# A new written order of all steps for a fused gated-attention and spatial-gating kernel on one core

## The chip, the core and the metric

The kernel runs on one core of a Trainium2 chip. The metric is the device time of one execution in microseconds (us); several runs are made and their median is compared. The core has a matrix engine (TensorE, PE in the profile; its weight loads are the separate row PEld), a vector engine (VectorE, DVE), an activation engine (ScalarE, ACT), a general one (GpSimd, POOL) and a queue engine (SyncE, SP) that issues all transfers here.

## What is computed

The first half is a gated linear attention over 4 batches, 8 heads, 768 tokens and 48 columns a head. The second half works on its output x, 768 tokens by 384 columns for each batch:

```python
f = 1 / (1 + exp(-f_logit))
for t in range(S):
    state = f[t][:, None] * state + outer(k[t], v[t])
    y[t] = q[t] @ state
h = relu(x @ w_in); u, v = h[..., :512], h[..., 512:]
v_n = (v - mean(v)) / sqrt(var(v) + 1e-6)
v_s = w_spatial @ v_n + b_spatial
out = (u * v_s) @ w_out
```

## The kernel before

The attention is cut into 24 units, numbered n = 0 to 23, of 128 tokens for all 8 heads: six units to a batch. The second half is cut by batch b, by half th of the tokens (384 each), by unit u inside the batch, and by column block c of 128. Every product in the second half is made as three products of a high and a low part (hi by hi and the two mixed ones).

The program is fully unrolled. Its order is a written list, PLAN, of 1176 steps; each step is a small function that issues one or a few instructions on one engine or one transfer on SP. Every engine works through its own instructions strictly in the order of the list, and waits by semaphores for what it needs from the others. So the list sets, for each engine, what stands behind what. A second list, BESIDES, names steps that take the other of two variants: c, r2 go to GpSimd instead of VectorE; sm goes to VectorE instead of GpSimd; ys goes to VectorE instead of ScalarE; for V, U, S and P it only swaps the second and third of the three products.

The steps that the texts below name, with their lines:

- Transfers on SP: LF:n gate logits of unit n (192 KB for the first eight units, L353, all of f, k and q, 768 KB, later), LK:n keys and queries (512 KB, L359), LQ:n values (192 KB, L363), LV and LU halves of w_in (768 KB, L294).
- Unit n: c (clamp, L367), e (exp and log, ACT L371 and L372), z (running sums: 16 matmuls for n under 8, L382, a DVE scan from n = 8), h and g (exponentials, ACT L388 and L393), k and q (scaled keys and queries, DVE L399 and L403), X (32 matmuls, scores and state update weights, L427), w (ACT copy, L433), m (DVE mask, L437), YS and kv (32 matmuls each, L479 and L451), r0, r1, r2 (state, L459, L465, L470), Yq (16 or 32 matmuls, L491), ys (output copy, L495), xt (3 transposes, L504), xh and xl (high and low part of x, ACT L515 and DVE L520).
- Weights: ca (ACT L303), ct (three DVE instructions, L308 to L310), ch and cl (high and low part, ACT L314 and DVE L320) turn words of a weight into two parts.
- Second half: V and U (9 matmuls each, L542 and L644), vr, bs, na, nb, nc, vn, vh, vl (normalisation; vl is the low part of v_n, L634), wh and wl (parts of w_spatial), S (18 matmuls, L658), P (the same product by sums of blocks for batches 2 and 3, 9 matmuls, L733), sm, sh, sl (gating and its parts), O (12 matmuls, L797), oc and od (copy out and store).

The tiles that bind the early transfers are few: three buffers `ins` for f, k, q of a unit, two `vals`, two `words`. LF:3 waits until k:0 and g:0 have read the f of buffer 0; LF:4 likewise for k:1; LK:3 waits for X:0; LQ:2 for kv:0. SP issues in list order, so one that waits holds all behind it.

Two lines of the loop that runs a step and of the variant test:

```python
def beside(name, *at):
    return name + ":" + ",".join(str(x) for x in at) in BESIDES
...
for what in PLAN[:stop]:
    ...
    run(what)
```

Of the kernel before, what the change touches and what calls it, by code (L numbers as in the profile page):

```python
# [29 lines left out]
P = 128  # L30
# [30 lines left out]
    xl:8 ch:O,1 r1:9 z:10 cl:O,1 bs:1,1 e:11 h:10 g:10 LW:2,1 sg:0,0,1 wh:2,1 wl:2,1 z:11 sm:0,0,1 sh:0,0,1 S:0,0,0  # L61
    k:10 sg:0,0,0 fm:9 r2:9 h:11 g:11 LF:12 q:10 k:11 S:0,0,2 sg:0,0,2 LW:1,1 wh:1,1 wl:1,1 bs:1,0 V:1,2 vr:1,2
    bs:1,2 na:1,0 X:10 w:10 LF:13 Yq:9 U:0,1,0 LQ:10 sl:0,0,1 m:10 q:11 sm:0,0,3 S:0,1,0 sg:0,1,0 ys:9 c:12 ur:0,1,0
    fm:11 sh:0,0,3 YS:10 sl:0,0,3 X:11 m:11 e:12 LF:14 nb:1,0 w:11 kv:10 LQ:12 xt:9 nc:1,0 r0:10 ur:0,0,2 xh:9 r1:10
    z:12 LO:0 r2:10 sm:0,0,0 S:0,1,3 sm:0,0,2 sg:0,1,3 vn:1,0 sh:0,0,0 sl:0,0,0 S:0,1,1 sg:0,1,1 sh:0,0,2 fm:10 h:12
    g:12 U:0,1,1 ur:0,1,1 sl:0,0,2 k:12 Yq:10 ys:10 c:13 e:13 YS:11 kv:11 r1:11 fm:12 q:12 X:12 LF:15 w:12 xl:9
    r0:11 c:15 z:13 m:12 h:13 Yq:11 ca:O,0 fm:13 xt:10 vn:1,2 ys:11 g:13 q:13 sm:0,1,0 S:0,1,2 YS:12 kv:12 c:14 e:14
    k:13 X:13 e:15 r0:12 Yq:12 xh:10 xt:11 xh:11 sg:0,1,2 ct:O,0 ch:O,0 xl:10 LQ:14 U:0,1,2 xl:11 cl:O,0 ur:0,1,2
    sm:0,1,2 sh:0,1,0 V:1,4 w:13 vh:1,2 r1:12 r2:12 z:14 h:14 fm:14 mr1 LQ:13 m:13 sm:0,1,1 O:0,0,0 oc:0,0,0
    od:0,0,0 vh:1,0 O:0,0,2 oc:0,0,2 g:14 k:14 O:0,0,1 YS:13 ys:12 od:0,0,2 sm:0,1,3 q:14 X:14 vl:1,2 vn:1,1 vh:1,1  # L70
    vl:1,1 m:14 sh:0,1,2 sl:0,1,2 sl:0,1,0 kv:13 V:1,5 vr:1,5 V:1,3 oc:0,0,1 vl:1,0 z:15 xt:12 sh:0,1,3 sl:0,1,3
    U:1,0,2 vr:1,4 r0:13 sh:0,1,1 bs:1,5 sl:0,1,1 O:0,1,2 bs:1,4 r1:13 r2:13 vr:1,3 xh:12 xl:12 O:0,1,0 w:14
    ur:1,0,2 LQ:15 O:0,1,1 bs:1,3 na:1,1 nb:1,1 nc:1,1 vn:1,3 vn:1,4 LF:16 c:16 h:15 g:15 k:15 vh:1,4 vh:1,3 Yq:13
    q:15 YS:14 ys:13 kv:14 r0:14 vn:1,5 vh:1,5 X:15 LF:18 vl:1,5 Yq:14 ys:14 oc:0,1,2 vl:1,3 vl:1,4 S:1,0,3 sg:1,0,3
    w:15 e:16 r1:14 r2:14 z:16 h:16 g:16 fm:16 S:1,0,2 LF:17 c:17 e:17 LQ:16 S:1,1,3 k:16 oc:0,1,0 sg:1,0,2 q:16
    U:1,0,3 ur:1,0,3 m:15 X:16 sg:1,1,3 m:16 fm:15 YS:15 kv:15 r0:15 r1:15 r2:15 U:1,0,0 ur:1,0,0 Yq:15 od:0,0,1
    z:17 S:1,1,2 S:1,0,1 U:1,0,1 w:16 h:17 g:17 sm:1,0,2 ys:15 k:17 oc:0,1,1 c:18 e:18 q:17 LF:19 sm:1,0,3 c:19 e:19
    z:19 sg:1,1,2 mr0 fm:17 h:19 X:17 w:17 ur:1,0,1 z:18 sh:1,0,2 sg:1,0,1 sm:1,0,1 sh:1,0,1 YS:16 kv:16 xt:13 xh:13
    r0:16 r1:16 r2:16 h:18 xl:13 g:18 LQ:17 xt:14 m:17 xt:15 S:1,0,0 k:18 Yq:16 q:18 YS:17 g:19 xh:14 ys:16 kv:17
    xl:14 X:18 r0:17 m:18 r1:17 Yq:17 sl:1,0,1 q:19 ys:17 U:1,1,2 xh:15 xl:15 k:19 ur:1,1,2 sm:1,1,2 w:18 S:1,1,0  # L80
    sg:1,1,0 LF:21 fm:18 c:21 sg:1,0,0 sm:1,0,0 sh:1,0,0 X:19 w:19 LQ:18 YS:18 kv:18 r0:18 r1:18 fm:19 xt:16 xt:17
    sh:1,1,2 xh:17 r2:18 sl:1,0,0 od:0,1,2 xl:17 od:0,1,0 sh:1,0,3 sl:1,0,3 S:1,1,1 sg:1,1,1 LF:20 e:21 xh:16 c:20
    LQ:20 m:19 e:20 z:20 V:2,0 h:20 fm:20 g:20 vr:2,0 sl:1,0,2 O:1,0,0 oc:1,0,0 k:20 LQ:19 xl:16 O:1,0,1 od:0,1,1
    LF:22 c:22 Yq:18 ys:18 sl:1,1,2 YS:19 kv:19 q:20 X:20 r0:19 Yq:19 r1:19 e:22 r2:19 LF:23 z:21 w:20 O:1,0,2 h:21
    g:21 U:1,1,1 ur:1,1,1 k:21 U:1,1,3 ur:1,1,3 U:1,1,0 fm:21 sm:1,1,3 z:22 sh:1,1,3 q:21 ys:19 ur:1,1,0 m:20 X:21
    c:23 e:23 oc:1,0,2 sm:1,1,0 m:21 z:23 sh:1,1,0 oc:1,0,1 YS:20 kv:20 LQ:21 V:2,1 vr:2,1 r0:20 r1:20 sl:1,1,3
    r2:20 w:21 bs:2,1 bs:2,0 V:2,2 h:22 fm:22 vr:2,2 g:22 k:22 U:2,0,1 ur:2,0,1 Yq:20 sm:1,1,1 YS:21 kv:21 LQ:23
    ys:20 q:22 X:22 r0:21 Yq:21 bs:2,2 na:2,0 sh:1,1,1 xt:19 xh:19 xl:19 xt:20 sl:1,1,1 xh:20 nb:2,0 nc:2,0 vn:2,2
    vh:2,2 vl:2,2 od:1,0,0 V:2,5 vr:2,5 r1:21 r2:21 V:2,3 vr:2,3 LQ:22 sl:1,1,0 h:23 O:1,1,0 xl:20 w:22 fm:23 bs:2,5
# [921 lines left out]
```

## Time and profile before

| quantity | value |
| --- | --- |
| median of three runs (lowest, highest) | 344.14 us (343.51, 344.34) |
| time of the profiled execution | 343.65 us |
| span of the profiled execution, first to last instruction | 341.9 us |
| PE busy | 327.2 us (96%) |
| DVE, ACT, POOL busy | 251.3, 181.9, 48.2 us |
| granted PE clock over the span | 0.997 |

The chain of waits gives start, length and what ran, as it ended last. A timeline row gives start, length, engine, line and the operation, with its output and input; x is how many instructions were merged, and brackets hold the idle time before and what ended it. A stretch row gives its bounds and length, then for each engine the busy time and in brackets the number of instructions, then the granted clock, the share of time that the DMA engines moved data, and GB/s. "issue" is time in which the engine waited for nothing that the profile shows. Queue q1 carries the transfers that SP issues; queue q8 carries packets of instructions.

### The profile page before, as it was taken

To read this page: it belongs to the slowest core of one execution; us is meant where nothing else is said; L and a number is where in the kernel's file an instruction comes from. 1 tells how busy PE (TensorE), PEld (TensorE's weight loads), DVE (VectorE), ACT (ScalarE), POOL (GpSimd) and SP (SyncE) were. 2 spreads that over 40 slices of the span, in tenths; PEclk is the share of its full clock that TensorE was granted. 3 is DMA by queue.
4 is the path that set the end of the run, shared out by engine and by line. 5 is a ranking of instruction groups with operands and counts; after the bars stand their busy time and mean duration, and the time that the engine had idled before them with its cause. 6 is when DMAs were issued, how large, how long until landed. Compare 5 with 4: busy or idle time off the path is not lost.

```text
span 341.9 us, 10491 instructions
## 1 busy us (share of the span) xinstructions
PE 327.2 (96%) x4554; PEld 304.7 (89%) x4554; DVE 251.3 (74%) x491; ACT 181.9 (53%) x369; POOL 48.2 (14%) x70
## 2 busy tenths in 40 slices
...
GB/s 253 353 97 269 182 271 304 252 30 138 143 157 134 83 54 110 77 157 117 2 143 265 46 85 50 46 200 104 71 1 0 2 0 0 2 46 49 23 74 98
DMA packets 16582, 38.38 MB, mean 112 GB/s; under 512 B 1552, under 2 KB 11792, under 8 KB 16528
## 3 DMA queue, kind: packets, MB, share of 16 engines
...
q14 instruction: 16, 0.13, 0.1%
HBM read 32.90 MB, written 4.72 MB: 110 GB/s over the span
## 4 chain that ended last, share of the span: by engine, by line
PE 93%; DMA 2%; issue 1%; DVE 1%; ACT 1%; SPq 0%; DVEq 0%
PE mm L658 15%; PE mm L644 12%; PE mm L542 12%; PE mm L797 10%; PE mm L733 7%; PE mn L733 6%; PE bp L427 6%; PE mn L797 5%; PE bp L479 4%; PE bp L491 4%; PE mn L542 3%; PE mn L644 3%; PE mm L504 3%; PE bp L451 3%; DMA words<-w_cv 2%; PE mm L382 2%
## 5 line engine op out<-in xcount | busy, mean ns | idle before, releaser
L399 DVE SCALAR_TENSOR_TENSOR fkq<-fkq 112x512 f32<-112x512 f32 x24 | 17.2, 718 | 11.4 <-ACT fkq L393 6.9
L649 ACT ACTIVATE uT<-mm 128x384 f32<-128x384 f32 x26 | 12.8, 491 | 22.8 <-PE mm L644 19.9
L779 ACT CAST gh<-uT 128x384 fp32r<-128x384 f32 x29 | 14.8, 514 | 18.3 <-DVE uT L775 13.6
L427 PE MATMUL bp<-q,fkq 48*64 48x112 f32 x768 | 23.7, 261 | 0.8 <-DVE q L403 0.6
L775 POOL TENSOR_TENSOR uT<-gt,uT 128x384 f32<-128x384 f32 x12 | 12.9, 1077 | 81.1 <-ACT uT L649 38.6
L470 POOL TENSOR_TENSOR sA<-sA,F 112x192 f32<-112x192 f32 x13 | 11.9, 916 | 85.4 <-DVE sA L465 81.2
L427 PEld LDWEIGHTS bp<-q,fkq 48*64 48x64 f32 x768 | 19.0, 133 | 4.7 <-DVE q L403 1.9
L377 DVE TENSOR_TENSOR_SCAN fkq<-runs,fkq 112x512 f32<-112x512 f32 x16 | 20.4, 1274 | 2.8 <-ACT fkq L372 2.8
L479 PEld LDWEIGHTS bp<-val,sc 64*64 64x64 f32 x768 | 14.2, 134 | 7.4 <-issue 3.5
L479 PE MATMUL bp<-val,sc 64*64 64x48 f32 x768 | 16.6, 220 | 4.1 <-DVE sc L437 2.1
L403 DVE TENSOR_TENSOR q<-fkq,F 112x512 f32<-112x512 f32 x24 | 16.5, 686 | 5.4 <-PE bp L491 4.0
L658 PE MATMUL mm<-w_sph,vnh 128*128 128x384 f32 x96 | 20.2, 345 | 0.0
L658 PE MATMUL mm<-w_sph,vnl 128*128 128x384 f32 x96 | 19.5, 338 | 0.0
L658 PE MATMUL mm<-w_spl,vnh 128*128 128x384 f32 x96 | 19.5, 338 | 0.0
L437 DVE TENSOR_TENSOR sc<-bp,mask 128x512 f32<-128x512 f32 x24 | 16.4, 683 | 3.8 <-PE bp L427 3.7
L644 PE MATMUL mm<-xTh,w_inh 128*128 128x384 f32 x78 | 18.9, 350 | 0.0
L367 POOL TENSOR_SCALAR fkq<-fkq 112x512 f32<-112x512 f32 (+1 forms) x8 | 12.4, 1550 | 40.7 <-DMA fkq<-fkq 20.6
L644 PE MATMUL mm<-xTl,w_inh 128*128 128x384 f32 x78 | 17.9, 338 | 0.0
L644 PE MATMUL mm<-xTh,w_inl 128*128 128x384 f32 x78 | 17.9, 338 | 0.0
L542 PE MATMUL mm<-w_inh,xTh 128*128 128x512 f32 x57 | 17.3, 411 | 0.0
L658 PEld LDWEIGHTS mm<-w_spl,vnh 128*128 128x128 f32 x96 | 17.1, 188 | 0.0
L658 PEld LDWEIGHTS mm<-w_sph,vnl 128*128 128x128 f32 x96 | 17.1, 188 | 0.0
(215 smaller groups left out, 900.3 us busy)
## 6 DMA issues: line engine op xcount, KB each, us to landing
...
val<-vv SPq DMA_DIRECT2D x24, 192.0 KB, 4.0
out<-osb SPq DMA_DIRECT2D x24, 192.0 KB, 2.1
fkq<-fkq SPq DMA_DIRECT2D x8, 512.0 KB, 5.7
...
fkq<-fn SPq DMA_DIRECT2D x8, 192.0 KB, 3.4
...
```

The costliest lines, as they stand in the source:

```text
L377: return nc.vector.tensor_tensor_scan(f[0:DP], runs, f[0:DP], 0.0, op0=ALU.mult, op1=ALU.add)
L399: nc.vector.scalar_tensor_tensor(k, f, 1.0 / F_LEAST, k, op0=ALU.min, op1=ALU.mult)
L403: nc.vector.tensor_tensor(qs[n % 2][:, :, :, 0:C], *(x.rearrange("p (j c t) -> p j c t", c=T // C, t=C) for x in (parts(n)[2], Fs[n % 2])) ...
L427: nc.tensor.matmul(sc[to, e, cs], k[dr, at:at + C], qs[n % 2][dr, j, chunk], start=True, stop=True)
L437: nc.vector.tensor_tensor(Ss[n % 2].rearrange("p (e j t) -> p e j t", e=2, t=C), scores(n)[:, :, :, 0:C], mask.unsqueeze(1).unsqueeze(1).b ...
L479: nc.tensor.matmul(y[to, e, cs], s[rows, keys[e]], v[rows, hd], start=j == 0, stop=False, skip_group_check=True)
L542: nc.tensor.matmul(acc, xs[:, c, ut * P:(ut + 1) * P], ws[:, c, G:FF], start=i == 0, stop=i == 3 * KX - 1)
L644: nc.tensor.matmul(acc[:, 0:TH], ws[:, kx, cs], xs[:, kx, :], start=i == 0, stop=i == 3 * KX - 1)
L658: nc.tensor.matmul(acc[:, 0:TH], vns.of((b, ks))[va][:, cs], w_sp_s[wb][:, ks, th * TH:(th + 1) * TH], start=i == 0, stop=i == 3 * KS - 1,)
L733: nc.tensor.matmul(mm.of(user)[:, 0:TH], x, y, start=n == ks == 0 and i not in (3, 6, 7), stop=n == ks == 2, skip_group_check=True,)
L779: nc.scalar.copy(gs.take((b, th, c), HU)[0], uTs.of((b, th, c)))
L797: nc.tensor.matmul(acc[:, ms], gs.of((b, th, c))[ga][:, ts], w_out_s[wb][:, c, ms], start=c == cs[0] == 0 and ga == wb == 0, stop=c == cs[ ...
```

## The change

Only the two lists change. The steps are the same 1176; their order is new from the beginning to the end, and 75 names in BESIDES differ (42 only before, 33 only after). In the first microseconds: LV:1, the first half of w_in for v, is issued as the fourth transfer instead of the fifth, ahead of LF:2; LQ:1 goes ahead of LQ:0, LK:2 ahead of LV:0, LK:3 behind LF:4; Yq:0 goes ahead of X:1 on PE; c:2 goes from POOL to DVE, ahead of ct:V,1; ys:0 from ACT to DVE. Up to V:0,2 the order on PE is otherwise unchanged.

```diff
 PLAN = """
-    LF:0 constants kz LF:1 kq:1 c:0 e:0 LF:2 kq:0 c:1 LK:0 e:1 z:0 g:0 k:0 h:0 q:0 c:2 kj e:2 LV:1 z:1 LQ:0 ca:V,1
-    ct:V,1 X:0 w:0 h:1 g:1 LK:1 z:2 ch:V,1 m:0 k:1 YS:0 kv:0 q:1 LF:3 c:3 e:3 LV:0 r0:0 r1:0 X:1 w:1 cl:V,1 g:2 r2:0
-    Yq:0 z:3 fm:0 h:2 LQ:1 m:1 YS:1 kv:1 LK:3 LK:2 ys:0 k:2 q:2 ca:V,0 xt:0 X:2 LF:4 c:4 r0:1 LQ:2 r1:1 xh:0 xl:0
-    e:4 z:4 m:2 g:3 LF:5 w:2 LK:4 r2:1 c:5 e:5 YS:2 kv:2 LQ:4 Yq:1 fm:1 h:3 ct:V,0 ys:1 ch:V,0 r0:2 q:3 z:5 g:5 g:4
-    k:3 xt:1 LQ:3 LU:0 r1:2 cl:V,0 r2:2 xh:1 xl:1 X:3 w:3 Yq:2 ys:2 V:0,1 k:4 fm:2 h:4 LF:7 LF:6 q:4 X:4 m:3 YS:3
-    c:6 kv:3 V:0,0 LK:5 ca:U,0 LU:1 ct:U,0 r0:3 w:4 ch:U,0 vr:0,1 xt:2 xh:2 m:4 YS:4 fm:3 r1:3 e:6 r2:3 vr:0,0 kv:4
-    h:5 Yq:3 LQ:6 xl:2 V:0,2 fm:5 ys:3 xt:3 z:6 c:7 cl:U,0 e:7 r0:4 k:5 ca:U,1 vr:0,2 q:5 X:5 LQ:5 r1:4 w:5 LK:6
...
+    LF:0 constants c:0 kz kq:1 e:0 kq:0 LF:1 z:0 c:1 e:1 h:0 fm:0 z:1 LK:0 q:0 g:0 k:0 X:0 LV:1 ca:V,1 LF:2 c:2 e:2
+    ct:V,1 h:1 fm:1 LK:1 w:0 LQ:1 m:0 z:2 LQ:0 YS:0 kv:0 q:1 g:1 k:1 LF:3 c:3 LK:2 g:2 r0:0 Yq:0 ch:V,1 X:1 e:3 z:3
+    cl:V,1 r1:0 LV:0 r2:0 LF:4 ca:V,0 c:4 h:2 fm:2 ys:0 m:1 YS:1 k:2 LK:3 LQ:2 LF:5 w:1 q:2 kv:1 r0:1 r1:1 r2:1 xt:0
+    xh:0 xl:0 X:2 e:4 m:2 LK:4 w:2 c:5 z:4 YS:2 kv:2 LQ:4 h:3 fm:3 LU:0 ct:V,0 Yq:1 e:5 z:5 g:3 k:3 ys:1 q:3 xt:1
+    r0:2 r1:2 ch:V,0 X:3 LQ:3 xh:1 Yq:2 cl:V,0 xl:1 g:4 k:4 r2:2 LF:7 V:0,1 w:3 ys:2 h:4 LK:5 ca:U,0 q:4 LF:6 X:4
+    m:3 YS:3 ct:U,0 w:4 kv:3 r0:3 g:5 r1:3 LU:1 V:0,0 xt:2 m:4 YS:4 kv:4 fm:4 LQ:6 ch:U,0 vr:0,1 cl:U,0 vr:0,0 xh:2
+    Yq:3 LQ:5 r2:3 h:5 c:6 fm:5 c:7 r0:4 e:6 r1:4 xl:2 e:7 V:0,2 ys:3 ca:U,1 vr:0,2 z:6 r2:4 h:6 q:5 z:7 LK:6 h:7
+    fm:6 fm:7 k:5 ct:U,1 X:5 Yq:4 w:5 m:5 LF:8 g:6 xt:3 k:6 ys:4 g:7 U:0,0,0 c:8 nm:0,0 YS:5 q:6 kv:5 X:6 r0:5 Yq:5
...
-    bs:0,5 na:0,1 k:9 fm:8 V:1,0 xt:7 xh:7 xl:7 wh:2,0 nb:0,1 LO:1 ca:O,1 U:0,1,3 nc:0,1 vn:0,4 X:9 vh:0,4 w:9
-    vn:0,3 YS:8 kv:8 r0:8 vl:0,4 V:1,1 m:9 vh:0,3 vl:0,3 LW:1,0 wh:1,0 vr:1,0 c:11 vn:0,5 vh:0,5 YS:9 kv:9 LQ:11
-    wl:1,0 Yq:8 ys:8 wl:2,0 r1:8 moe vr:1,1 vl:0,5 ur:0,1,3 S:0,0,3 r2:8 xt:8 r0:9 sg:0,0,3 e:10 ct:O,1 S:0,0,1 xh:8
...
+    U:0,0,2 k:9 wl:0,1 q:9 X:9 nb:0,1 xh:7 LW:1,0 nc:0,1 w:8 xl:7 vn:0,3 vh:0,3 m:9 LQ:9 vn:0,5 LB V:1,1 LF:11
+    wh:1,0 fm:9 w:9 vn:0,4 YS:8 wl:2,0 vh:0,4 kv:8 wl:1,0 moe YS:9 kv:9 r0:8 vh:0,5 Yq:8 vl:0,5 vl:0,4 vl:0,3
+    S:0,0,0 vr:1,0 LO:1 ca:O,1 e:10 c:11 ct:O,1 vr:1,1 z:10 r1:8 ch:O,1 cl:O,1 fm:8 sg:0,0,0 ys:8 sm:0,0,0 S:0,0,3
...
 BESIDES = """
-    c:2 r2:0 r2:1 r2:2 c:6 V:0,0 ys:5 U:0,0,1 U:0,0,3 V:0,4 c:10 V:0,5 U:0,0,2 r2:7 V:1,1 r2:8 S:0,0,1 sm:0,0,1
-    S:0,0,0 r2:9 U:0,1,0 sm:0,0,3 S:0,1,0 c:15 sm:0,1,0 U:0,1,2 r2:12 sm:0,1,1 r2:13 ys:14 r2:14 S:1,1,3 S:1,1,2
...
+    r2:0 c:4 ys:0 r2:1 r2:2 ys:4 c:8 V:0,3 r2:6 U:0,0,1 V:0,4 V:0,5 U:0,0,3 c:9 r2:7 V:1,1 S:0,0,0 sm:0,0,0 S:0,0,3
+    r2:8 sm:0,0,3 r2:9 S:0,0,1 S:0,1,1 S:0,1,0 sm:0,0,1 c:13 U:0,1,1 r2:10 sm:0,1,1 S:0,1,3 ys:11 U:0,1,2 sm:0,1,3
...
```

## Rows read from the trace of the kernel before

**Rows 1.** The page's busy time, share of the span and instructions by engine.
```profile
PE 327.2 (96%) x4554; PEld 304.7 (89%) x4554; DVE 251.3 (74%) x491; ACT 181.9 (53%) x369; POOL 48.2 (14%) x70
```

**Rows 2.** The chain of waits, first 80 us: start, length, what ran.
```profile
2.65 7.09 DMA words<-w_cv
...
17.55 1.64 issue
...
23.69 0.39 issue
...
26.74 0.99 PE bp L427 x32
...
32.55 0.47 issue
...
37.37 2.29 PE mm L542 x9
...
74.19 3.37 PE mm L658 x18
```

**Rows 3.** Stretches: PE, PEld, DVE, ACT, POOL busy and count, clock, DMA, GB/s.
```profile
10.00:20.00 10.00, 6.12 (x220) 5.08 (x212) 8.16 (x14) 6.58 (x12) 1.22 (x2) 1.00 0.79 286
20.00:30.00 10.00, 8.94 (x240) 7.37 (x238) 8.77 (x16) 7.65 (x16) 1.84 (x4) 1.00 0.47 150
...
0.00:17.50 17.50, 9.88 (x221) 8.16 (x221) 9.84 (x19) 13.02 (x24) 4.56 (x15) 1.00 0.84 299
...
19.10:24.00 4.90, 3.90 (x126) 3.20 (x127) 3.92 (x8) 3.33 (x8) 0.65 (x2) 1.00 0.50 152
```

**Rows 4.** The timeline of PE around its first pauses.
```profile
13.37 0.68 PE L479 MATMUL bp<-val,sc 64*64 64x48 f32 x32 [2.08 <-DVE sc L437]
...
17.11 0.43 PE L479 MATMUL bp<-val,sc 64*64 64x48 f32 x13
19.18 0.49 PE L479 MATMUL bp<-val,sc 64*64 64x48 f32 x18 [1.64 <-issue]
```

**Rows 5.** DMA queues in 13:16.9, 16.92:17.93, 20:21.7, 21.7:22.65 us: packets, MB, share.
```profile
q1 hardware_dynamic: 604, 1.50, 99.3%
...
q8 instruction: 1, 0.02, 6.2%
...
q1 hardware_dynamic: 156, 0.53, 98.4%
...
q8 instruction: 1, 0.02, 6.1%
```

**Rows 6.** DMA share, 24 to 27 us in 40 slices; the lone 9 is q8.
```profile
DMA  0000000000000000900000004488967674630010
```

**Rows 7.** The timeline of SP: the transfers issued around two pauses.
```profile
10.33 0.80 SPq L359 DMA_DIRECT2D fkq<-fkq  x2
...
18.27 0.33 SPq L353 DMA_DIRECT2D fkq<-fn  x1
18.70 0.38 SPq L359 DMA_DIRECT2D fkq<-fkq  x1
```

**Rows 8.** DMA issues at 1.72 and 2.18 us: count, KB, us to landing.
```profile
fkq<-fn SPq DMA_DIRECT2D x1, 192.0 KB, 3.4
...
fkq<-fkq SPq DMA_DIRECT2D x1, 512.0 KB, 5.6
```

**Rows 9.** The timeline of DVE from the first conversion of w_in.
```profile
9.77 0.56 DVE L308 TENSOR_SCALAR words<-words 128x768 int32<-128x768 int32 x1 [0.28 <-DMA words<-w_cv]
10.74 0.98 DVE L309 SCALAR_TENSOR_TENSOR words<-words 128x768 int32<-128x768 int32 x1 [0.41 <-ACT words L303]
...
12.63 0.68 DVE L437 TENSOR_TENSOR sc<-bp,mask 128x512 f32<-128x512 f32 x1
...
14.43 0.35 DVE L367 TENSOR_SCALAR fkq<-fkq 128x384 f32<-128x384 f32 x1
```

**Rows 10.** DVE alone, 9.77 to 76.20 us: length, busy time, count.
```profile
9.77:76.20 66.43, 58.45 (x112) 1.00 0.65 220
```

More of the change, by code (lines that the diff above doesn't have):

```diff
@@ L60 @@
-    wl:1,0 Yq:8 ys:8 wl:2,0 r1:8 moe vr:1,1 vl:0,5 ur:0,1,3 S:0,0,3 r2:8 xt:8 r0:9 sg:0,0,3 e:10 ct:O,1 S:0,0,1 xh:8
[L61 to L89, printed above, removed]
```

99 lines of the change are left out of this document (63 added, 36 removed).

## The prediction

> **What bounds the kernel now.** Begin with the busy times: PE works 327.2 us [rows 1] of a span of 341.9, so 14.7 us are all that an order can win as long as the matmuls stay the same. The stretches say where these lie: from 10 to 20 us PE idles 3.9 us, from 20 to 30 us 1.1 us [rows 3]; the first 4.9 us wait for the first input and some 3.8 us at the end for the last stores, and both lists keep these. After 33 us PE is busy without a break, so what is won before then is won at the end, if nothing new waits later. The chain of waits then shows what PE's early idle time is. Three pieces of it are "issue": 1.64 us at 17.55, 0.39 at 23.69, 0.47 at 32.55 [rows 2]. In the timeline of PE the first lies in the middle of YS:1, after 13 of its matmuls [rows 4]: no data can be missing there, since the same step went on before and after it.
>
> The instruction queue explains it. From the start to that pause PE runs 221 matmuls and as many weight loads, and from there to the next pause some 126 of each [rows 3], so pauses come at every 128 or so. A packet of q8 lies ahead of each: 16.92 to 17.93 us, and 21.7 to 22.65 [rows 5]; PE goes on 1.25 us after the first has ended and 1.4 after the second (at 19.18 and 24.08). So PE's instructions come in blocks, and PE stops where the next is not there yet.
>
> When is a block asked for? If two blocks lie ready, then when PE steps from one into the next: for the first at 221 - 128 = 93 matmuls, the first ones of YS:0, about 13.6 us; for the second at 19.18; for the third at 24.08. The packets start 3.3, 2.5 and 1.1 us later. The third met an empty queue [rows 6]; ahead of the first two the transfers keep the DMA engines at 99% and 98% [rows 5]. I read this as a wait behind what SP had issued before: LK:3 and LK:2, 512 KB each, issued from 10.33 us, for the first; LF:5 and LK:4, issued at 18.27 and 18.70, for the second [rows 7].
>
> The Trainium skill, page "Runtime: NRT & Kernel Launch", section "Instruction fetch mechanics", describes blocks of 16 KiB, but calls the crossing of a boundary mostly hidden and gives PE room for 2,048 instructions. The trace disagrees here: 1.64 us stand open after 442. By the page nothing would be won there, and the sum below would be 0.35 us in place of 1.9.
>
> Behind PE stands DVE: from 9.77 to 76.20 us, where the sixth vl of batch 0 is done, it works 58.5 of 66.4 us, and idles 7.9 [rows 10].
>
> **The change, part by part.**
>
> *Loads.* LK:0 and LV:1 move up one issue each (0.45 us) and LF:2 falls behind them. Today LF:2 lands at 1.72 + 3.4 = 5.1 us, LK:0 at 7.8 [rows 8], LV:1 at 2.65 + 7.1 = 9.75 [rows 2]. LV:1 now lands at 9.3 at the latest (the issue step alone). At the earliest it is 0.5 us earlier still, 8.8: so long LF:2's 192 KB take at the 0.385 MB a us of a full queue (1.50 MB in 3.9 us) [rows 5], and they are no longer ahead. The same 0.5 us then puts LF:2 between 9.3 and 9.8; I take 9.4, since both savings hold where the queue is full.
>
> *VectorE up to YS:0.* c:2 (0.35 us) [rows 9] now lies on DVE ahead of ct:V,1 and waits for LF:2. So ct:V,1 starts at 9.4 + 0.4 = 9.8, no sooner than today's 9.77; but its second instruction, which today waits 0.41 us for ACT's ca:V,1 [rows 9], no longer does, since LV:1 was there half a us before. m:0 comes at 12.3 in place of 12.63, and YS:0, which PE has waited for 2.08 us [rows 4], at 13.0 in place of 13.37. Gain 0.35; bounds 0 (LF:2 at 9.8) and 0.45 (at 9.3). Without this cover the clamp would cost its 0.35.
>
> *X:1 behind Yq:0.* Yq:0 needs r0:0, which on DVE comes after m:0, q:1, k:1 and c:3. At 0.6 to 0.7 us each for the first three (L437 as measure) [rows 9] and 0.35 for c:3 and r0:0, r0:0 ends near 14.95, Yq:0 (16 matmuls, 0.6) near 15.55. X:1 was ready by 14.2 and has to wait in PE's line: it ends at 16.5. DVE fills the wait with cl:V,1, r1:0 and the new ys:0; m:1 ends at 17.3 and YS:1 starts at 17.4, against 17.11 today [rows 4]. So the 0.35 is lost and 0.3 more: a term of -0.65, bounds -0.9 and 0 (X:1 is then hidden by the block's wait).
>
> *The first block.* It is asked for at 13.2. LK:3, which lies ahead of the packet today, now waits on SP behind LF:4, and that waits for k:1, 14.2 us. What is ahead is LV:0 and what came before it, 0.52 MB less than today, 1.35 us at 0.385 MB a us: the packet starts near 16.93 - 1.35 = 15.6. Bounds: 14.3 (1.1 us after the request, an empty queue) and 16.9 (as today). With the 2.25 us from packet start to go-on (16.93 to 19.18), PE can go on at 17.85, and comes there at 17.65. Of 1.64 us some 0.15 stay: gain 1.5; bounds 0.7 and 1.64.
>
> *The second and third.* The second is asked for at 17.85. LF:5 waits for k:2, which on DVE follows m:1, and is issued at 18.0 to 18.1, LK:4 0.4 later, and their packets start later than that. So the request, behind both today, is now ahead: 1.1 to 1.6 us, not 2.5, and the 0.39 goes: gain 0.39, bounds 0 and 0.39. The third block finds an empty queue as today; the fourth is asked for in Yq:2 and has LU:0 ahead, as today, but LU:0 is now issued before LQ:3, so it ends sooner: the 0.47 goes too, bounds 0 and 0.47. Where the stalls go, DVE is late next: X:3 (today 26.74 [rows 2]) waits for ct:V,0, k:3 and q:3 behind m:2, and these are moved earlier by the same steps.
>
> *The low part of unit 2.* V:0,2 needs xl:2 for its last product; ahead of it on DVE c:6, which was on POOL, comes new with its 0.35. I take half: -0.15, bounds -0.35 and 0.
>
> *The rest.* PE's switches between the small attention matmuls and the big ones are 32 in both lists, so its stream costs the same. LK:2 ahead of LV:0, LQ:1 ahead of LQ:0, ys:0 from ACT to DVE: nothing; LQ:0 lands before 12.5, ahead of YS:0, and the rest behind other work; without that cover LQ:0 would hold YS:0 us for us. The end has the same O, oc and od behind the last matmul.
>
> Sum: 0.35 - 0.65 + 1.5 + 0.39 + 0.47 - 0.15 = 1.9 us, with bounds -0.5 and 3.0. Against the profiled execution's 343.65 that is 341.75. The median of the runs is 0.5 above it, so the forecast is **342.2 us**. V:0,2 (today 37.37 [rows 2]) should start near 35.4.
>
> **The rivals.** A measurement of this kernel can tell 0.3%, 1.03 us, from no change.
>
> *A: the blocks stay late.* The packet may wait its turn for another reason than the transfers ahead of it. For that: PE's way to the first boundary is the same 221 matmuls. Against it: the third packet came after 1.1 us from an empty queue. Then 0.35 and little more: 343.7. Chance 0.13, of which 0.04 is the page's reading, by which the pause is something that no order touches.
>
> *B: DVE is late at S:0,0,0 (slower).* S now opens with its vl product second (BESIDES), so vl:0,3, the last of the six on DVE, is needed 9 of its 18 matmuls after the start, 1.7 us; today S:0,0,3 (at 74.19, 3.37 us [rows 2]) asks for the vl third. PE can be there at 74.2 - 1.9 = 72.3, so the last must be done by 74.0. DVE has 0.5 us less to do (kj, ys:5 and three others out, c:2, c:6 and others in): from 9.8 to 74.0 it may idle 64.2 - 58.0 = 6.2 us; today it idles 7.9 [rows 10], 3.1 of that between 10 and 30 us [rows 3], where the pauses of PE make it wait, and I expect 2 of these gone. If all 7.9 stay, 1.7 us of the gain are lost (343.9); from 6.2 + 1.9 + 1.0 = 9.1 on the kernel is slower than today by over 1.03, and at 10 it takes 346.0. Chance 0.15: 0.05 no change, 0.10 slower.
>
> *C: the conversion starts no earlier.* LF:2 at 9.8 or later: YS:0 stays at 13.4, YS:1 at 17.75, but the queue empties as told and the block's pause goes all the same. Gain 1.2 to 1.5: 342.8. Chance 0.12, half of it over and half under 1.03 us once one more pause of 0.4 stays.
>
> **How the numbers follow.** The forecast has 0.60, nearly all of it faster. Faster 0.60 + 0.06 = 0.66; same 0.13 + 0.05 + 0.05 = 0.23; slower 0.10 and 0.01 of C with a late B: 0.11. The forecast's own range is 341.1 (the upper bounds together, 3.0) to 343.0. The range that should hold 8 in 10 goes from 340.9 to 344.6: above it lies B's slower part, 0.10, and below it little.
>
> **What would show it.** YS:0 at 13.0 (12.5 to 13.4); the first q8 packet before 16.2 with LK:3 issued after 14; no pause over 0.4 us in YS:1; the second packet ahead of LK:4; X:3 near 25; V:0,2 near 35.4; PE without idle at the first S. Wrong would be: a q8 packet that starts no earlier though the queue ahead is shorter (A); PE waiting for vl near 72 us (B); VectorE waiting for LF:2 past 9.8 (C).

## The result and the profile after

Slower: the median of 14 runs of the changed kernel is 347.68 us (344.26 to 349.17), against 343.72 us for 14 runs of the kernel before beside them; the ratio is 1.0091, 95% interval 1.0062 to 1.0119. The quotient of the two medians is larger, 1.0115: the changed kernel's runs fall into two groups, six from 344.3 to 346.2 us and eight from 347.7 to 349.2, and the median and the profiled execution lie in the upper one. Of all runs below two count as slow and are left out of their ratio, 348.92 and 348.23 us of the kernel called "The store first"; with them it would be about 1.004. Forecast were 342.2 us, 340.9 to 344.6. The profiled execution took 347.68 us, its span is 346.0 us, 4.1 more than before. Line numbers are one smaller than before (the list is one line shorter), and one smaller again in the kernels of the experiments.

The page's busy line and granted clock answer to [rows 1]: PE has 3.0 us more to do, in the same 4554 matmuls, and the clock row has a 6 and a 7 in the slices from 8.7 to 26 us, where the kernel before has only nines.

```profile
PE 330.2 (95%) x4554; PEld 306.9 (89%) x4554; DVE 252.6 (73%) x492; ACT 182.2 (53%) x369; POOL 44.8 (13%) x69
...
PEclk9679999999999999999999999999999999999999
```

**The head.** The stretches of 5 us (columns as in [rows 3]) show where: the granted clock is 0.63 and 0.50, half of 2.4 GHz, and back at 0.84 and 1.00 behind it.

```profile
10.00:15.00 5.00, 3.38 (x74) 2.77 (x68) 4.52 (x8) 4.18 (x8) 0.91 (x1) 0.63 0.91 316
15.00:20.00 5.00, 4.52 (x94) 4.08 (x88) 3.55 (x9) 3.30 (x6) 1.92 (x3) 0.50 0.67 216
20.00:25.00 5.00, 4.38 (x121) 3.50 (x117) 3.31 (x9) 2.19 (x5) 0.64 (x2) 0.84 0.52 147
```

The timeline of PE, to be held against [rows 4]: it stands 1.57 us ahead of z:2, and z:2 then takes 1.97 us (1.09 before); YS:0 starts at 13.88, not 13.0, and YS:1 (20.54) runs through its 32 matmuls in one go. The pause of 1.64 us is gone, but PE arrives 3.4 us later than before.

```profile
11.87 1.97 PE L381 MATMUL mm<-tri,fkq 128*64 128x128 f32 x16 [1.57 <-ACT fkq L371]
13.88 1.10 PE L478 MATMUL bp<-val,sc 64*64 64x48 f32 x32
...
20.54 1.11 PE L478 MATMUL bp<-val,sc 64*64 64x48 f32 x32
```

ScalarE and VectorE show what z:2 waits for: the first instruction of the V conversion (L302, ca:V,1) waits for LV:1 until 9.84, and e:2 (L370) stands behind it on ScalarE; on VectorE c:2 (L366) waits for LF:2 until 10.34, and the conversion (L307) and m:0 stand behind that ([rows 9]: 9.77 and 12.63; now 10.62 and 13.14).

```profile
9.84 0.90 ACT L302 ACTIVATE words<-words 128x768 f32<-128x768 f32 x1 [1.75 <-DMA words<-w_cv]
10.74 0.52 ACT L370 ACTIVATE fkq<-fkq 128x384 f32<-128x384 f32 x1
```
```profile
10.34 0.36 DVE L366 TENSOR_SCALAR fkq<-fkq 128x384 f32<-128x384 f32 x1 [1.10 <-DMA fkq<-fn]
```

V:0,0 starts at 34.13 us, against 33.25 before: 0.9 us lost, where 1.9 were forecast to be won. This is one execution: in six other traces below the same head starts V:0,0 between 31.1 and 33.1 us, and in two others the old head does at 33.15 and 33.93.

**Behind it.** From 35 us to the end the view of waits lists none of PE in the kernel before. Now it waits 1.28 us ahead of X:15, 0.46 ahead of X:17, and 0.15 for instructions inside S:0,0,0:

```profile
76.78 0.97 PE L657 MATMUL mm<-w_sph,vnl 128*128 128x384 f32 x4 [0.15 <-issue]
...
145.07 1.00 PE L426 MATMUL bp<-q,fkq 48*64 48x112 f32 x32 [1.28 <-ACT vnh L622]
...
167.35 1.00 PE L426 MATMUL bp<-q,fkq 48*64 48x112 f32 x32 [0.46 <-DVE fkq L398]
```

Each step is measured from its start to the start of the next, against the kernel before or, for the two S, the kernel with all four edits below. So these places cost 0.40 us (S:0,0,0: 3.68 in place of 3.28), 1.21 (kv:14 up to X:15: 1.81 in place of 0.60) and 0.54 + 0.29 (S:1,0,3 up to X:17: 3.80 in place of 3.26; X:17 up to YS:16: 1.11 in place of 0.82), together 2.4. With the 0.88 of the head that is 3.3 us; the last matmul ends 3.2 us later than before (341.35, 338.14). The last 0.9 us are behind the last matmul: 4.65 us to the end of the span, 3.76 before.

The wait at X:15 begins on SP. LF:17 (768 KB) is issued at 133.21, the store od:0,0,1 right behind it at 133.59, and it lands after 5.7 us; the page's median for such a store is 2.1.

```profile
133.21 0.33 SPq L354 DMA_DIRECT2D fkq<-fkq  x1
133.59 0.43 SPq L817 DMA_DIRECT2D out<-osb  x1
```
```profile
out<-osb SPq DMA_DIRECT2D x1, 192.0 KB, 5.7
```

There are three osb buffers, so ScalarE's fourth copy, oc:0,1,2, needs this one free, and stands 4.01 us. Behind it on ScalarE are vh:1,3, h:15 and g:15; VectorE stands 3.54 us for the vh, and k:15 and q:15, which X:15 needs, come last: q:15 ends at 144.97 us, X:15 starts at 145.07.

```profile
134.53 0.46 ACT L812 COPY osb<-mm 128x384 f32<-128x384 f32 x1
...
139.41 0.48 ACT L812 COPY osb<-mm 128x384 f32<-128x384 f32 x1 [4.01 <-DMA out<-osb]
139.79 0.64 ACT L622 ACTIVATE vnh<-vr 128x512 fp32r<-128x512 f32 x1
```
```profile
140.45 0.69 DVE L633 TENSOR_TENSOR vnl<-vr,vnh 128x512 fp32r<-128x512 f32 x1 [3.54 <-ACT vnh L622]
...
144.29 0.68 DVE L402 TENSOR_TENSOR q<-fkq,F 112x512 f32<-112x512 f32 x1
```

The wait at X:17 begins on GpSimd, to which the change moved c:19. It starts 0.01 us behind VectorE's scan z:18 and takes 2.49 us; e:19 on ScalarE stands 2.57 us for it, with g:17 behind it, and k:17 behind that.

```profile
161.62 1.23 DVE L376 TENSOR_TENSOR_SCAN fkq<-runs,fkq 112x512 f32<-112x512 f32 x1 [1.56 <-ACT fkq L371]
161.63 2.49 POOL L366 TENSOR_SCALAR fkq<-fkq 112x512 f32<-112x512 f32 x1 [8.90 <-DMA fkq<-fkq]
...
164.16 0.63 ACT L370 ACTIVATE fkq<-fkq 112x512 f32<-112x512 f32 x1 [2.57 <-POOL fkq L366]
```

### The profile page after: what moved, and what is told of

It is laid out like the page before. It is cut to its first block, busy times and chain, and to the rows that moved or that the text cites. A ratio compares the mean times of both kernels' runs of the same rounds, so it can differ in the third digit from the quotient of the medians.

```text
span 346.0 us, 10472 instructions
## 1 busy us (share of the span) xinstructions
PE 330.2 (95%) x4554; PEld 306.9 (89%) x4554; DVE 252.6 (73%) x492; ACT 182.2 (53%) x369; POOL 44.8 (13%) x69
## 4 chain that ended last, share of the span: by engine, by line
PE 85%; DMA 7%; ACT 3%; DVE 2%; issue 1%; POOL 1%; SPq 0%; ACTq 0%; POOLq 0%
PE mm L541 13%; PE mm L657 12%; PE mm L643 10%; PE mm L796 10%; PE mn L732 7%; PE mm L732 5%; PE bp L426 5%; PE mn L643 4%; DMA words<-w_cv 4%; PE bp L478 4%; PE bp L490 3%; PE mn L796 3%; PE mm L503 3%; PE bp L450 2%; PE mm L381 2%; DMA out<-osb 2%
## 5 line engine op out<-in xcount | busy, mean ns | idle before, releaser
L426 PE MATMUL bp<-q,fkq 48*64 48x112 f32 x768 | 25.0, 267 | 2.8 <-DVE fkq L398 1.3
L426 PEld LDWEIGHTS bp<-q,fkq 48*64 48x64 f32 x768 | 20.0, 136 | 7.0 <-DVE fkq L398 1.8
L782 DVE TENSOR_TENSOR gl<-uT,gh 128x384 fp32r<-128x384 f32 x30 | 16.3, 559 | 9.6 <-ACT gh L778 9.6
L402 DVE TENSOR_TENSOR q<-fkq,F 112x512 f32<-112x512 f32 x24 | 16.9, 703 | 5.9 <-DMA fkq<-fkq 3.5
L541 PE MATMUL mm<-w_inh,xTh 128*128 128x512 f32 x66 | 20.0, 410 | 0.0
L541 PE MATMUL mm<-w_inh,xTl 128*128 128x512 f32 x66 | 19.0, 396 | 0.0
L541 PE MATMUL mm<-w_inl,xTh 128*128 128x512 f32 x66 | 18.9, 395 | 0.0
L381 PE MATMUL mm<-tri,fkq 128*48 128x128 f32 (+1 forms) x128 | 11.5, 342 | 7.2 <-ACT fkq L371 7.2
L812 ACT COPY osb<-mm 128x384 f32<-128x384 f32 (+1 forms) x20 | 9.4, 469 | 16.0 <-PE mm L796 11.9
L370 ACT ACTIVATE fkq<-fkq 112x512 f32<-112x512 f32 (+1 forms) x24 | 14.3, 594 | 6.2 <-DVE fkq L366 3.5
L432 ACT COPY W<-bp 128x384 f32<-128x384 f32 x24 | 11.5, 479 | 11.0 <-PE bp L426 10.1
```

The lines of the kernel that those rows point to most:

```text
L381: nc.tensor.matmul(z[lo:hi, j * T:(j + 1) * T], f[:, at:at + hi - lo], tri, start=True, stop=True)
L402: nc.vector.tensor_tensor(qs[n % 2][:, :, :, 0:C], *(x.rearrange("p (j c t) -> p j c t", c=T // C, t=C) for x in (parts(n)[2], Fs[n % 2])) ...
L426: nc.tensor.matmul(sc[to, e, cs], k[dr, at:at + C], qs[n % 2][dr, j, chunk], start=True, stop=True)
L541: nc.tensor.matmul(acc, xs[:, c, ut * P:(ut + 1) * P], ws[:, c, G:FF], start=i == 0, stop=i == 3 * KX - 1)
```

## The experiments

Theory M: the loss lies in these waits of the new list behind the head. Theory H: it lies in the head (late LF:2, half clock), and the rest costs nothing. All ratios are against runs of the kernel before beside them. "Starts" are those of a step's first matmul on PE.

**New head, old rest.** The steps up to the old V:0,0 in the new order, all others in the old one.

```diff
+ the new list's order for every step that stands up to V:0,0 in the old list
  the old list from there on
```

> The new order and variants for the steps that the old list has up to V:0,0 (33 us), the old list from there on. Theory M (the loss lies in waits after 75 us: PE behind ACT at 143.8 us, behind POOL's clamp at 166.6): V:0,0 begins near 34.1 as in the new kernel and the end is 0.6 to 1.0 us later than before, ratio 1.002 to 1.003. Theory H (the loss is the late LF:2 and the granted clock of 0.5 from 11.9 to 21.4 us): ratio 1.007 to 1.010, as the whole change.

Ratio 1.0033 (1.0008 to 1.0059). With the same head the clock stayed at 1.00 up to 35 us in the profiled execution: YS:0 starts at 12.99, YS:1 at 17.13, V:0,0 at 31.18, 2.1 us earlier than before. Then the seam costs: VectorE stands 2.71 us for LF:6, which the new list issues late, with ct:U,0 and m:4 behind it, and V:0,2 comes 1.5 us later than before (38.80, 37.30).

```profile
32.34 0.36 DVE L365 TENSOR_SCALAR fkq<-fkq 128x384 f32<-128x384 f32 x1 [2.71 <-DMA fkq<-fn]
```

So by the two ratios about a third of the loss comes with the new head (0.0033 of 0.0091). In this trace all of it belongs to the seam, since the head itself was early.

**Old head, new rest.**

```diff
+ the old list's order for every step that stands up to V:0,0 in the new list
  the new list from there on
```

> The old order and variants for the steps that the new list has up to V:0,0, the new list from there on. Theory M: clock 1.0 throughout, V:0,0 near 33.3, but the waits near 143 and 166 us are there, and the kernel is slower than before by 2.0 to 2.5 us, ratio 1.006 to 1.007. Theory H: no difference from before, ratio 0.999 to 1.002.

Ratio 1.0102 (1.0062 to 1.0142): the whole loss, with the old head and a clock of 1.00. H falls. The waits of the rest are all there (kv:14 up to X:15 1.89 us, S:1,0,3 up to X:17 3.79, X:17 up to YS:16 1.11), and the one in S:0,0,0, which theory M had not counted, is large:

```profile
77.53 1.14 PE L656 MATMUL mm<-w_sph,vnl 128*128 128x384 f32 x5 [1.71 <-issue]
```

**LF:2 back.**

```diff
- LF:1 z:0 ... LV:1 ca:V,1 LF:2 c:2
+ LF:1 LF:2 z:0 ... LV:1 ca:V,1 c:2
```

> The new kernel, LF:2 issued ahead of LK:0 again and LV:1 fifth, as before; nothing else moved. If LF:2 behind the weights is what idles PE (10.3 to 11.87 us) and drops the clock: LF:2 lands near 5.1, z:2 starts by 10.4, the clock stays at 1.0, V:0,0 starts 0.9 us earlier than in the new kernel (33.2), and the pause in YS:1 is back in part, since PE gets to the block's edge sooner. Theory M: the end 0.5 to 0.9 us sooner than the new kernel, ratio to before 1.006 to 1.008. Theory H: ratio 0.998 to 1.001.

Ratio 1.0077 (1.0048 to 1.0107). z:2 still starts at 11.63, since e:2 stands behind ca:V,1 on ScalarE whenever its input comes; the clock fell to 0.50 again. The place of LF:2 was the smaller part of the delay. V:0,0 starts at 33.05, near the 33.2 expected, but that lies inside the spread of the unedited head.

**Matmuls in the gap.** Sixteen matmuls on zeros (step D of the kernel, a bank of its own, no result used) behind X:0.

```diff
- constants c:0 kz kq:1
+ constants c:0 kz kj kq:1
- X:0 LV:1
+ X:0 W0 D:16 W1 LV:1
```

> The new kernel with 16 matmuls of 256 columns on a tile of zeros between X:0 and z:2, where PE waits for LF:2 (their result is not used; the zero fill of that tile is moved to the start). They take some 1.7 us. If it is PE's idle time there that lets the granted clock fall, it stays at 1.0, z:2 takes 1.0 us and not 2.0, and V:0,0 starts at 33.0 to 33.8. Theory M: ratio to before 1.006 to 1.008. Theory H: 0.998 to 1.002. If the clock falls all the same, V:0,0 stays at 34.1 or later.

Ratio 1.0274 (1.0228 to 1.0321). Every 5 us stretch from 5 to 40 us has a clock of 1.00, and V:0,0 starts at 31.32. But the clock held up to 35 us without these matmuls too (new head and old rest, and c:19 late below), so this one trace does not show that they hold it. And with 16 matmuls more in its stream PE stands for instructions at three new places, in Yq:3, V:0,3 (1.06 us at 49.55) and Yq:8:

```profile
36.76 0.25 PE L489 MATMUL bp<-sB,q 48*64 48x48 f32 x1 [1.31 <-issue]
...
78.11 0.26 PE L489 MATMUL bp<-sA,q 48*64 48x48 f32 x2 [3.05 <-issue]
```

So it is no mend, and whether work in the stand ahead of z:2 holds the clock is not shown.

The next four kernels are the changed kernel with one edit each, and with all of them.

**The store first.**

```diff
- O:0,0,2 X:14 LF:17 c:17 ur:1,0,1 oc:0,0,1 od:0,0,1
+ O:0,0,2 X:14 ur:1,0,1 oc:0,0,1 od:0,0,1 LF:17 c:17
```

> The changed order with the 768 KB load LF:17 and its c:17 moved behind the first output store od:0,0,1, so that the store no longer queues behind the load. Theory M (the loss sits in three waits of the new middle): od:0,0,1 lands in about 2 us instead of 5.75, ScalarE's copy oc:0,1,2 no longer stands 4.0 us, and the 1.4 us excess before X:15 goes: X:15 ends up 1.2 to 1.5 us earlier against V:0,0, and the time falls by about as much (346.3, ratio to the kernel before 1.005). Rival R (nothing is gained, the next late thing takes over, for instance c:17 now late): X:15 gains under 0.4 us and the time stays at 1.009.

Ratio 1.0025 (0.9999 to 1.0051). The store, issued alone, lands in 1.9 us, and oc:0,1,2 now waits for its matmuls only:

```profile
out<-osb SPq DMA_DIRECT2D x1, 192.0 KB, 1.9
```
```profile
135.92 0.48 ACT L811 COPY osb<-mm 128x384 f32<-128x384 f32 x1 [2.48 <-PE mm L795]
```

kv:14 up to X:15 takes 0.69 us in place of 1.81. The first wait is shown, and nothing took its place. What it is worth in time is told only roughly: the changed kernel's ratio is 1.0091 above and 1.0055 when it is run again below.

**c:19 behind X:17.**

```diff
- c:18 e:18 z:18 c:19 kj q:17 e:19 g:17 z:19 S:1,0,3 k:17 X:17
+ c:18 e:18 z:18 kj q:17 g:17 S:1,0,3 k:17 X:17 c:19 e:19 z:19
```

> The changed order with c:19, e:19 and z:19 moved behind X:17. In the changed kernel ScalarE stands 2.57 us before e:19 for GpSimd's c:19 (2.49 us), with g:17 and so k:17 and X:17 queued behind it. Theory M: the excess at S:1,0,3 (0.57) and X:17 (0.31 to 0.8) goes, 0.8 to 1.2 us, ratio about 1.006. Rival R: the wait only moves to X:18 or X:19, which need e:19 in their turn; under 0.3 us, ratio 1.009.

Ratio 1.0049 (1.0019 to 1.0079). S:1,0,3 and X:17 run without a wait. But this trace alone proves little: c:19 took 1.49 us in it, and with 1.49 the wait is absent without the edit too (next kernel). In S:0,0,0, which PE reached at 71.82, 3.1 us earlier than in the changed kernel, it stood for its instructions:

```profile
74.82 0.97 PE L656 MATMUL mm<-w_sph,vnl 128*128 128x384 f32 x4 [1.33 <-issue]
```

**A late store moved up.**

```diff
- oc:2,1,0 sh:3,1,3 ... od:3,0,1 od:2,1,0 od:3,0,2
+ oc:2,1,0 od:2,1,0 sh:3,1,3 ... od:3,0,1 od:3,0,2
```

> The changed order with one output store, od:2,1,0, moved from the last line of the list right behind its copy oc:2,1,0, so that its osb buffer comes free before the last three copies need it. Theory M: the copy that stood 2.00 us for a store near the end no longer stands, and the tail after the last matmul falls from 4.65 to about 3.8 us: 0.8 us, ratio 1.0065. Rival R: the last copy waits for the last matmul only, and the tail is the last two stores one behind another: no change, 1.009.

Ratio 1.0062 (1.0032 to 1.0093). ScalarE's copy no longer stands 2.00 us for a store, but the last copy waits for the last matmul in both, and starts right at its end. From that copy's end to the end of the span it is 3.5 us here and 4.3 in the changed kernel; in the kernel with all four edits, which ends in the same order, it is 4.3 again, so executions of one order differ by as much. Rival R was right that the last copy waits for the last matmul only. Whether the order plays a part stays open: from the last matmul to the end of the span it is 3.8 to 4.6 us in the seven traces with the store moved, 4.4 to 5.1 in the seven with the new end as it was, and 3.8 and 3.9 in the two with the old end. The ratio cannot tell it either.

```profile
333.86 0.48 ACT L811 COPY osb<-mn 128x384 f32<-128x384 f32 x1 [1.28 <-issue]
...
338.57 0.32 ACT L811 COPY osb<-mm 128x192 f32<-128x192 f32 x1 [1.02 <-PE mm L795]
```

**All four edits.** The three above, and V:1,1 between the steps of small matmuls ahead of S:0,0,0: 96 of them follow one another there, not 160.

```diff
- V:1,1 LF:11 wh:1,0 fm:9 w:9 vn:0,4 YS:8 wl:2,0 vh:0,4 kv:8
+ LF:11 wh:1,0 fm:9 w:9 vn:0,4 YS:8 wl:2,0 vh:0,4 kv:8 V:1,1
```

> The edits of the three kernels above together, and the two groups of V:1,1 put between YS:8, kv:8 and YS:9 as in the order before, so that no more than 80 small matmuls follow one another before S:0,0,0. Theory M: 1.4 + 0.9 + 0.8 + 0.4 = 3.5 us off, so about 344.1, ratio 1.000 (0.997 to 1.003); the head's own gain is not paid out because the clock falls in it. Rival R (the waits are only where the slack of a tightly packed order shows, and move on): under 1.2 us off, ratio 1.006 or more.

Ratio 0.9989 (0.9966 to 1.0012): the loss is gone. What each edit is worth by itself the ratios do not tell, since their intervals overlap, and the move of V:1,1 was not run alone. S:0,0,0 runs through without a stand, and so do X:15 and X:17, the latter although c:19 lost its race to the scan again:

```profile
158.95 1.23 DVE L375 TENSOR_TENSOR_SCAN fkq<-runs,fkq 112x512 f32<-112x512 f32 x1 [1.56 <-ACT fkq L370]
158.98 2.48 POOL L365 TENSOR_SCALAR fkq<-fkq 112x512 f32<-112x512 f32 x1 [8.91 <-DMA fkq<-fkq]
```

That is what the kernel with c:19 alone could not tell: a clamp of 2.48 us and no wait.

**The changed kernel again.** No edit.

> The changed kernel itself again, for a second trace. Theory M: the wait before X:15 (1.4 us), the copy that stands for a store near the end and a late first block at S:0,0,0 are there again, since they follow from the order; the wait at X:17 is there only if GpSimd's c:19 takes about 2.5 us and not 1.5. Rival (the waits are chance of one execution): at least two of the first three are gone. Ratio to the kernel before 1.007 to 1.010 either way.

Ratio 1.0055 (1.0020 to 1.0091). The wait ahead of X:15 (kv:14 up to X:15 1.86 us, the copy stands 4.08) and the one in S:0,0,0 (3.68) follow from the order: both steps are as long as in the first trace to 0.05 us. The one at X:17 is not, and c:19 started ahead of the scan this time:

```profile
159.80 1.49 POOL L365 TENSOR_SCALAR fkq<-fkq 112x512 f32<-112x512 f32 x1 [8.63 <-DMA fkq<-fkq]
...
160.04 1.45 DVE L375 TENSOR_TENSOR_SCAN fkq<-runs,fkq 112x512 f32<-112x512 f32 x1 [1.56 <-ACT fkq L370]
```
```profile
137.84 0.48 ACT L811 COPY osb<-mm 128x384 f32<-128x384 f32 x1 [4.08 <-DMA out<-osb]
```

V:0,0 starts at 32.73, 1.4 us earlier than in the first trace of the same kernel: LF:2 landed 0.3 us earlier, and the clock fell later, in 15 to 20 us (0.66). The two traces of one kernel differ by 2.4 us at the last matmul: 1.4 of it up to V:0,0, where the clock and the loads decide, and 0.5 between X:15 and X:17, where the race of c:19 does. The stand of 0.47 us in kv:3 [rows 2], gone in the first trace, is back here:

```profile
32.51 0.29 PE L449 MATMUL bp<-val,W 64*48 64x48 f32 x5 [0.52 <-issue]
```

**Old head, mended rest.**

```diff
+ the old list's order for every step that stands up to V:0,0 in the new list
  the list with all four edits from there on
```

> The kernel with all four edits, but with the steps up to V:0,0 in the order of the kernel before. It tells what the new head is worth once the rest is mended. Theory P (the new head pays its 1.9 us only when the clock holds, and it mostly does not): V:0,0 ends at the old 33.2, and the time is that of the four edits with the new head within 0.8 us, 342.6 to 344.2, ratio 0.997 to 1.001. Rival (the new head pays on the whole): 1.5 to 2 us slower than with it, 345.0, ratio 1.004.

Ratio 0.9983 (0.9949 to 1.0017). With the same rest the old head is as good as the new one (0.9989): what the head was changed for shows no gain that these runs can tell, each ratio being good to some 0.3%.

Up to S:0,0,0 this kernel differs from "Old head, new rest" in the place of V:1,1 alone. PE comes there at nearly the same time (74.53 and 74.32 us), and where it stood 1.71 us for instructions it now runs through. So the move of V:1,1 takes that stand away:

```profile
75.69 1.22 PE L656 MATMUL mm<-w_sph,vnl 128*128 128x384 f32 x6
```

The old head is not safe from slow matmuls either: here z:2 took 1.97 us and YS:0 1.10, as in the changed kernel at half the clock, though the clock reads 1.00 in this trace, and V:0,0 started at 33.93.

```profile
11.47 1.97 PE L380 MATMUL mm<-tri,fkq 128*64 128x128 f32 x16
```

**LF:2 first, and the V conversion behind e:2 and k:1** (in the kernel with all four edits).

```diff
- LF:1 z:0 ... LV:1 ca:V,1 LF:2 c:2 e:2 ct:V,1 h:1 ... k:1 LF:3
+ LF:1 LF:2 z:0 ... LV:1 c:2 e:2 ca:V,1 h:1 ... k:1 ct:V,1 LF:3
```

> The kernel with all four edits, and in the head LF:2 right behind LF:1, ca:V,1 behind e:2 and ct:V,1 behind k:1, so that neither z:2 nor m:0 and YS:0 wait behind the conversion of the V weights. Theory P: z:2 starts by 10.6 and YS:0 by 12.0, TensorE does not stand over 1.5 us there, the granted clock stays 1.0, V:0,0 comes at 30.5 to 31.2 instead of 33.1, and the time falls 1.5 to 2 us below that of the four edits: about 341.7, ratio 0.994. Rival L (the loads set the pace of the head, whose DMA share is 0.9 to 1.0 up to 15 us): YS:0 at 12.8 or later, ratio 0.998 or more. Rival N (the head comes early, but the next waits take it): V:0,0 by 31.2 and the time still 343.

Ratio 1.0085 (1.0047 to 1.0123), slower than without it. I had put the conversion's 2.5 us on VectorE ahead of r0:0, which Yq:0 needs, and the head's worst stand of all came of it:

```profile
17.36 0.77 PE L489 MATMUL bp<-sB,q 48*64 48x48 f32 x10 [3.13 <-DVE sB L455]
```

**LV:1 later as well.**

```diff
- LV:1 c:2 e:2 ca:V,1 h:1 fm:1 LK:1 w:0 LQ:1 m:0 z:2 LQ:0
+ c:2 e:2 h:1 fm:1 LK:1 LQ:0 w:0 LQ:1 LV:1 ca:V,1 m:0 z:2
```

> As the kernel above with LF:2 first, and the 768 KB load LV:1 behind LK:1, LQ:0 and LQ:1 as well, with ca:V,1 behind it. Theory L (loads set the pace): LK:1 and LQ:0 land by 8, X:1 and YS:1 come earlier, V:0,0 by 30.3, ratio 0.993. Theory P: the same as the kernel above, since LF:2 was the load that mattered; ratio 0.994. Rival: the conversion of V,1 now runs at 13 to 17 us on VectorE, ahead of sB and sA of the next steps, and X:2 comes no earlier; V:0,0 at 31 to 32, ratio 0.997.

Ratio 1.0078 (1.0047 to 1.0109), with the same stand (Yq:0 at 17.27). V:0,0 starts at 35.82 and 34.48 us in the two. Neither of the two told loads from order, so two more followed, with the conversion behind m:1.

**The conversion behind m:1.**

```diff
- m:0 z:2 LQ:0 YS:0 kv:0 q:1 g:1 k:1 LF:3 c:3 ... ch:V,1 X:1 e:3 z:3 cl:V,1 r1:0 ... m:1 YS:1
+ m:0 h:1 fm:1 z:2 LQ:0 YS:0 kv:0 q:1 g:1 k:1 ca:V,1 LF:3 ... X:1 r1:0 c:3 e:3 z:3 ... m:1 ct:V,1 ch:V,1 ... ys:0 YS:1 cl:V,1
```

Beside these two lines LF:2 goes behind e:1, and ca:V,1 and ct:V,1 leave their places ahead of m:0.

> The kernel with all four edits, and in the head LF:2 behind e:1, w:0 ahead of h:1, and the conversion of V,1 (ca:V,1, ct:V,1, ch:V,1, cl:V,1) moved behind m:1 on VectorE and behind g:1 on ScalarE, so that m:0, r0:0 and m:1 do not wait for it. Theory P (the stands behind the conversion, and the clock that falls in them, cost the head's gain): YS:0 by 12.2, Yq:0 by 14, no stand of TensorE over 1.5 us between 10 and 20 us, V:0,0 by 30.8, and the time 1.5 to 2 us under that of the four edits: 341.8, ratio 0.994. Rival L (the loads): YS:0 at 13 or later, X:2 at 20 or later, ratio 0.998 to 1.001. Rival N: V:0,0 early and the ratio still 0.998.

Ratio 1.0139 (1.0097 to 1.0180). YS:0 starts at 13.59 and V:0,0 at 37.86, not by 12.2 and 30.8; the clock fell to 0.67 in 10 to 15 us and to 0.50 in 20 to 25.

**The same, LV:1 later.**

```diff
- X:0 LV:1 c:2 e:2 w:0 LK:1 LQ:1 m:0 h:1 fm:1 z:2 LQ:0
+ X:0 c:2 e:2 w:0 LK:1 LQ:0 LQ:1 LV:1 m:0 z:2 h:1 fm:1
```

> As the kernel above, and the 768 KB load LV:1 behind LK:1, LQ:0 and LQ:1. Theory L: X:1 and YS:1 come 0.5 to 1 us earlier than there, V:0,0 by 30.2, ratio 0.993. Theory P: as there, 0.994. Rival: V:0,1 now waits for cl:V,1; V:0,0 no earlier than 31.5, ratio 0.997.

Ratio 1.0085 (1.0056 to 1.0114). On the queue LV:1 goes behind LK:1, LQ:0 and LQ:1, and LQ:0 ahead of LQ:1; the order on each engine is the same. YS:0 starts 1.6 us earlier than there (13.59): 0.9 of it is there at z:2 (10.80, 11.70), the rest is z:2 itself, 1.09 us at the full clock in place of 1.97. This one shows both halves: YS:0 starts at 11.95 and X:1 at 13.75, 2.3 us earlier than with the four edits alone (16.09). Then PE stands three times: for e:3, which stands behind c:3 and r1:0, and twice for what is queued behind the conversion, for ys:0 behind ct:V,1 and for w:1 behind ch:V,1 and ca:V,0. The clock falls, and X:2 comes at 22.44 (21.44 with the four edits).

```profile
15.98 1.97 PE L380 MATMUL mm<-tri,fkq 128*64 128x128 f32 x16 [1.05 <-ACT fkq L370]
18.73 1.10 PE L477 MATMUL bp<-val,sc 64*64 64x48 f32 x32 [0.79 <-DVE ysb L493]
20.78 0.90 PE L449 MATMUL bp<-val,W 64*48 64x48 f32 x32 [0.94 <-ACT W L431]
```
```profile
15.00:20.00 5.00, 3.07 (x48) 2.51 (x48) 4.43 (x7) 2.65 (x5) 0.55 (x2) 0.59 0.55 207
```

So loads do set a part of the pace of YS:0, and the conversion, 3.4 us of VectorE and 1.7 of ScalarE for V,1 alone, sets that of what follows: at each place that I tried it stands in front of a step that PE waits for.

None of these kernels beats the kernel before by more than its interval. The best two, with all four edits, are at 0.9989 and 0.9983.

## Why the prediction was wrong

The step that failed is the one called *The rest*, with its sentence "LK:2 ahead of LV:0, LQ:1 ahead of LQ:0, ys:0 from ACT to DVE: nothing", and the premise above it, that what is won before 33 us is won at the end "if nothing new waits later". It was put at 0, though the whole list was new, c:19 was moved to POOL and V:1,1 away from its place. It measured 2.4 us in the profiled execution (1.21 + 0.83 + 0.40). From V:0,0 to the last matmul PE takes 304.9 us in the kernel before, 307.2 and 306.2 in the two traces of the changed kernel, 309.4 with the old head and the new rest, and 305.0 with all four edits. In the runs it is about 1%: old head and new rest 1.0102, mended 0.9983. These places could have been found in the diff: a 768 KB load ahead of a store whose buffer the fourth copy needs, a clamp on POOL ahead of e:19, 160 small matmuls in a row ahead of S. (The same paragraph counts 32 switches between small and big matmuls in both lists; counted from the steps, X, YS, kv, Yq against V, U, S, P, O, they are 51 in both, so they are equal all the same.)

*Loads* was sized at its early end. In the profiled execution LV:1 landed at 9.8, no earlier than before, and LF:2 at 10.3, not 9.4; that is rival C, and worse than I put it: YS:0 at 13.88, 0.5 us later than before. But with the same order LF:2 landed at 9.4 and 9.5 us in two of the other traces and between 9.7 and 10.1 in the rest, and YS:0 started between 12.9 and 13.7. The old head spreads as well: YS:0 at 13.37, 13.71 and 13.81 in three traces. One trace of each kernel was too few for terms of 0.35 us. *VectorE up to YS:0* followed c:2 on VectorE only; e:2 on ScalarE, behind ca:V,1, was not in it, and z:2 waits for that.

*The blocks*, the largest terms, were right. The first packet of q8 started at 16.03 us (forecast 15.6, "before 16.2"), LK:3 was issued at 15.51, and behind it came no pause in YS:1. That alone says little, as PE came to YS:1 3.4 us late; but where the clock held (new head, old rest) the packet started at 14.34, YS:1 at 17.13, and no pause came either. The 0.39 us of [rows 2] is gone in both traces of the changed kernel, the 0.47 in the first alone (0.52 in the second). Rival A falls. Where the clock held, the whole sum of the head came out: V:0,0 started at 31.18, 31.32 and 31.08 us in the three traces with 1.00 from 5 to 35 us (new head and old rest, matmuls in the gap, c:19 late), and at 31.32 in one where it was back by 16 us (a late store moved up). That is 1.9 to 2.2 us earlier than before; forecast were 1.9 at V:0,2.

What the sum did not hold is the clock. In the profiled execution the removed pauses were paid back by matmuls at half rate: z:2, YS:0, X:1, z:3, YS:1 took 1.97, 1.10, 1.72, 1.97 and 1.11 us, and z, X and YS take 1.09, 1.00 and 0.68 at the full clock, together 3.3 us more.

*Rival B* had the right place and the wrong cause. PE does stand in S:0,0,0, but for instructions, not for vl: with c:19 late the last vl of the batch is done at 72.90 us, and PE stands up to 74.82. It is a pause like those that the change takes out of YS:1 and YS:2, and with the new head it stood longer where PE arrived earlier (0.15 us from 74.96, 0.51 from 72.48 with the late store moved up, 1.33 from 71.82 with c:19 late). So S:0,0,3 starts at 76.68 with c:19 late and at 76.52 with the late store moved up, where V:0,0 was 2.0 and 1.7 us earlier than with the four edits, and at 77.20 there: of 2 us, 0.5 to 0.7 are left.

The end ("the same O, oc and od") is open: two traces of the same end differ by 0.8 us there, as much as the 0.9 behind the last matmul, yet none of the seven with the new end as it was is under 4.4; whether the order has a share is not shown.

Still open too: a trace in which the clock holds and S:0,0,0 has no stand was not seen, so whether the head's 2 us would then reach the end is not shown. In the trace with the store first V:0,0 came 1.3 us earlier than before (31.92) and the last matmul 0.7 (337.42); the medians and ratios (0.9989 with the new head, 0.9983 with the old) show no gain on the average. And why the changed kernel's runs fall into two groups, 2 to 3 us apart, is shown in part only, by the two traces above.
